# Fillers on TensorE moved from early pauses to later ones, written into the PSUM bank of the product that follows

## The chip, the cores and the metric

The kernel runs on one core of a Trainium2 chip. The metric is the device time of one execution in microseconds (us). Three timed runs of the kernel before gave 224.25, 225.02 and 223.09 us; their median is 224.25 us.

## The reference

Two blocks follow each other. The first is a linear attention with a sketched feature map, the second a phase mixer over tokens. Cut to what matters:

```python
# q, k, v: (4, 4, 1088, 32); S1, S2: (8, 32)
def phi(x):                       # 64 features of each row
    a = einsum('rd,bhsd->bhsr', S1, x); b = einsum('rd,bhsd->bhsr', S2, x)
    return einsum('bhsi,bhsj->bhsij', a, b).reshape(..., 64)
q_p, k_p = phi(q), phi(k)
kv  = einsum('bhsf,bhsd->bhfd', k_p, v);  z = k_p.sum(axis=2)
num = einsum('bhsf,bhfd->bhsd', q_p, kv); den = einsum('bhsf,bhf->bhs', q_p, z) + 1e-6
x = (num / den) heads put side by side    # (4, 1088, 128)

theta = x @ w_theta
zr, zi = x * cos(theta), x * sin(theta)
y = einsum('ts,bsd->btd', w_tok_r, zr) + einsum('ts,bsd->btd', w_tok_i, zi)
u = x + y
out = u + maximum(u @ w_ch, 0)            # (4, 1088, 128)
```

## The kernel before, in words

The kernel is written as a list of 1015 operations. Each has an engine (P for TensorE, V for VectorE, A for ScalarE, G for GpSimd, S for the queue of SyncE), the buffers that it writes and reads, and a function that issues its instructions. The order in which they are issued is written out by hand in `ORDER`, and the slot of every buffer in `PLACES`; nothing is planned at run time. Each engine works through its own operations in that order. An operation waits by semaphores for its operands and for the last reader of a slot that it takes over. PSUM has eight slots, `ps0` to `ps7`, each one bank of 512 float32 columns.

The work is staged by batch. Keys are transposed and turned into features (`kT`, `kf`), summed with the values (`kv`), and their Gram matrix (`sums`, `rest`) goes through a chain of small products (`chain`) that gives the scales for the exact slicing of the query side. `CHAINS` treats batch 0, batch 1, and batches 2 and 3 together. Queries are sliced (`q0`), multiplied (`levels`), divided by the denominator (`den`), brought to the output of the attention (`num`), and then the angles (`theta`) and the token mixing (`mix` for batches 0 and 1, `winograd` for 2 and 3) follow, then the last product and the stores (`out`). The token matrix arrives in 17 row blocks of float64 words, which ScalarE and VectorE turn into float32 (lines 555 to 561).

Fillers are matrix products on a tile of zeros, `idle`, whose result nobody reads. `spin` (line 349) issues one: bfloat16, 128 x 384, into the PSUM tile `nowhere` in slot `ps0`. Ten of them run at the start (line 353). `SPINS` names operations by their number and says how many fillers `issue` puts right ahead of each. One more filler is an operation of its own (line 1289): it waits for the key sums of batch 0, is the last that uses `nowhere`, and after it slot `ps0` goes to other tiles.

The operations that `SPINS` names in either version, all on TensorE:

| number | what it is | line of its instructions |
|---|---|---|
| 76 | transposes of the first key group, batch 0 | 694 |
| 89 | Gram matrix of the rounded keys, batch 0 | 637 (by 312) |
| 72 | key features, second group, batch 0 | 704 (by 312) |
| 303 | transposes of a query group, batch 0 | 918 |
| 111 | product with ones in the chain of batch 0 | 807 (by 312) |
| 172 | the product `second` in the chain of batch 1, into a tile `np` in `ps1` | 798 to 800 (by 312) |
| 174 | product with ones in the same chain, into a tile `pt` in `ps2` | 807 (by 312) |
| 1010 | last transpose of `finish_turned`, batch 2, into a tile `ut` in `ps5` | 1134 |

Line 312 is the helper `mm`, through which most products are issued. Around operation 172, TensorE's own order is: key features of batch 1 (141), then 172, transposes of the first query products of batch 0 (441, 439; line 1010), 174, key and value sums of batch 1 (144), the first numerators (443), further transposes and numerators, angles (459, 460) and, after 187, the levels of batch 1 (521). The operand of 172 is `tac`, which VectorE's operation 170 (line 788) and ScalarE's 171 (line 782) finish. At the end of the order stand 1006, 1010 and 1011 on TensorE, with copies on ScalarE (1007, 1012), the last additions on VectorE and the stores.

Of the kernel before, what the change touches and what calls it, by code (L numbers as in the profile page):

```python
# [9 lines left out]
F32 = mybir.dt.float32  # L10
# [11 lines left out]
P = 128  # L22
# [54 lines left out]
    "2 0 1 5 0 5 0 2 3 4 0 2 5 2 5 "  # L77
)
SPINS = (
    "76:2 89:4 72:2 303:1 111:2 "  # L80
)
WARM = 0
SPLIT = ()
# [35 lines left out]
class Layout:  # L119
# [5 lines left out]
    def buf(self, cls, shape, dt, name):  # L125
        b = Buf(cls, shape, dt, name)
        self.bufs.append(b)
        return b

    def op(self, eng, dur, fn, w=(), r=(), lk=0, fly=0.0, half=False, n=0):  # L130
        o = Op()
        o.n = n
        o.lk, o.fly, o.stage, o.half = lk, fly, self.stage, half
        o.i, o.eng, o.dur, o.fn = len(self.ops), eng, dur, fn
        pred = set()
        o.bufs = []

        def parts(x):
            return x if isinstance(x, tuple) else (x, None)

        def hits(table, b, key):
            t = table.get(b, {})
            return [v for k, v in t.items() if k is None or key is None or k == key]

        for x in r:
            b, key = parts(x)
            pred.update(hits(self.last_w, b, key))
            o.bufs.append(b)
        for x in w:
            b, key = parts(x)  # L150
            pred.update(hits(self.last_w, b, key))
            for s in hits(self.readers, b, key):
                pred.update(s)
            o.bufs.append(b)
        for x in r:
            b, key = parts(x)
            self.readers.setdefault(b, {}).setdefault(key, set()).add(o.i)
        for x in w:
            b, key = parts(x)
            if key is None:  # L160
                self.last_w[b] = {None: o.i}
                self.readers[b] = {}
            else:
                self.last_w.setdefault(b, {})[key] = o.i
                self.readers.setdefault(b, {})[key] = set()
        o.bufs = list(dict.fromkeys(o.bufs))
        for b in o.bufs:
            b.ops.append(o.i)
        pred.discard(o.i)
        o.pred = sorted(pred)  # L170
        self.ops.append(o)
        return o
# [10 lines left out]
    def issue(self, pools, fill):  # L183

        spins = dict(tuple(map(int, x.split(":"))) for x in SPINS.split())
        for o in self.order:
            for _ in range(spins.get(o.i, 0)):
                fill()
            for b in o.bufs:
                if b.ap is None:  # L190
                    b.ap = view(pools[b.cls](b.slot), b.shape, b.dt)
            o.fn()


WORD = {F32: 4, I32: 4, U32: 4, BF16: 2, F16: 2, I16: 2, I64: 8}
# [2 lines left out]
def view(raw, shape, dt):  # L198
    n = math.prod(shape)
    t = raw[:, : n * WORD[dt] // 4]  # L200
    if dt != F32:
        t = t.bitcast(dt)
    if len(shape) > 1:
        names = " ".join(f"a{i}" for i in range(len(shape)))
        t = t.rearrange(f"p ({names}) -> p {names}", **{f"a{i}": s for i, s in enumerate(shape)})
    return t
# [19 lines left out]
def kernel(  # L226
# [12 lines left out]
    B, _, NC, H, D = q.shape  # L239
# [13 lines left out]
    GW = GC * P  # L253
# [18 lines left out]
    def maker(c, width):  # L272
        pool = banks if c == "ps" else room
        return lambda i: pool.tile([P, width], F32, tag=f"{c}{i}", name=f"{c}{i}")

    pools = {c: maker(c, w) for c, (_, w) in classes.items()}
    L = Layout(classes)
    op, buf = L.op, L.buf
# [4 lines left out]
    V, A, G, T, SY = nc.vector, nc.scalar, nc.gpsimd, nc.tensor, nc.sync  # L283

    def fixed(shape, dt, name):
        b = Buf(None, shape, dt, name)
        n = math.prod(shape) * WORD[dt]
        b.ap = view(const.tile([P, (n + 3) // 4], F32, tag=name, name=name), shape, dt)
        return b
# [56 lines left out]
    idle = fixed((GW,), BF16, "idle")  # L346
    nowhere = buf("ps", (GW,), F32, "nowhere")

    def spin():
        T.matmul(nowhere(), idle()[:, 0:P], idle(), start=True, stop=True, skip_group_check=True)  # L350

    op("G", 0.3, lambda: G.memset(idle(), 0.0), [idle], [])
    op("P", 1.73, lambda: [spin() for _ in range(10)], [nowhere], [idle])
    op("V", 1.55, constants, [hm, bdm, halfpi, ups, steps, upv, ones], [])
    op("A", 0.72, lambda: A.activation(warm(), halfpi(), AF.Sin), [warm], [halfpi])
# [46 lines left out]
    def powers(mfn, m, n, name):  # L402
# [7 lines left out]
        def inv():  # L410
# [16 lines left out]
                                    op=ALU.max, apply_absolute_value=True), [m2], [(sp, 0)])  # L427
# [152 lines left out]
    kvb, kk, kg = {}, {}, {}  # L580
# [260 lines left out]
    def chain_out(bs):  # L841
        nu = nus[bs]
        at("kvb", bs[0])
        for n, b in enumerate(bs):
            mk = buf("sm", (H,), F32, "mk")
            ep[b] = (nu, n)
            op("V", 0.16, lambda n=n, mk=mk: tt(V, mk(), nu()[:, 0, n * H:(n + 1) * H], bde(), ALU.mult), [mk], [nu, bde])
            tr = buf("ps", (P,), F32, "kvtr")
            kt = kvb[b]
            bd = buf("sm", (H, D), F32, "kvbd")  # L850

            def twice(tr=tr, kt=kt):
                for n in range(2):
                    mm(tr()[n * R * R:(n + 1) * R * R], kt(), ident(), True, True)

            op("P", 0.31, twice, [tr], [kt, mk], half=True)
            vop(P, lambda bd=bd, tr=tr, mk=mk: tt(V, bd(), tr().rearrange("p (h d) -> p h d", h=H),
                                                  bc(mk(), 2, [P, H, D]), ALU.mult), [bd], [tr, mk])
            kvb[b] = bd
# [12 lines left out]
    def query_scale(b):  # L872
        at("qscale", b)
        x = ld["q", b]
        m = buf("sm", (3,), F32, "qm")
        n = NC * HD
        f = qx[b] = buf("big", (n,), F32, "qx")
        if QGRAM[b]:
            pq = buf("ps", (HW,), F32, "pq")
            dg = buf("sm", (HW,), F32, "qd")  # L880

            def gram():
                for c in range(NC):
                    y = x()[:, c].rearrange("p h d -> p (h d)")
                    for n in sides:
                        mm(pq()[n], y[:, n], y[:, n], c == 0, c == NC - 1)

            op("P", 1.05, gram, [pq], [x], half=True)
            op("V", 0.3, lambda: V.tensor_tensor_reduce(dg(), pq(), idh(), 1.0, 0.0, ALU.mult, ALU.add, m()[:, 0:1]),
               [dg, m], [pq, idh])  # L890
        else:
            op("A", act(n) + 0.1, lambda: A.activation(f(), x().rearrange("p c h d -> p (c h d)"), AF.Square,
                                                       accum_out=m()[:, 0:1]), [f, m], [x])
        t = buf("ps", (1,), F32, "qt")
        op("P", 0.25, lambda: mm(t(), ones(), m()[:, 0:1], True, True), [t], [m])
        s = qs[b] = fixed((2,), F32, f"qs{b}")

        def scale():
            a = m()[:, 1:2]
            ts(a, t(), QFIX, ALU.mult, TINY, ALU.max)  # L900
            ai = a.bitcast(I32)
            ts(ai, ai, 1, ALU.logical_shift_right, EXPO, ALU.bitwise_and)
            ts(ai, ai, EXPO, ALU.bitwise_xor)

        op("V", 0.53, scale, [m], [t])
        op("A", 0.2, lambda: A.mul(s()[:, 0:1], m()[:, 1:2], 2.0**-49), [(s, 0)], [m])
        small(lambda: ts(s()[:, 1:2], s()[:, 0:1], s()[:, 0:1], ALU.mult, ec()[:, 1:2], ALU.mult, eng=G), [(s, 1)],
              [(s, 0), (ec, 1)], dur=0.8)
# [372 lines left out]
    for bs in CHAINS:  # L1281
        for b in bs:
            kfeatures(b)
            key_sums(b)
            query_scale(b)
        chain(bs)
        chain_out(bs)
        if not bs[0]:
            op("P", 0.1, spin, [nowhere], [kvb[WARM]] if WARM < B else [idle])
    for b in range(B):  # L1290
        query_slices(b)
    for i in range(NK):
# [20 lines left out]
    with tc.manual_schedule():  # L1313
        L.issue(pools, spin)
# [43 lines left out]
```

## Time and profile before

| | before |
|---|---|
| timed runs, us | 224.25, 225.02, 223.09 (median 224.25) |
| profiled execution: time, us | 223.05 |
| profiled execution: span from first to last instruction, us | 221.3 |
| mean granted TensorE clock | 0.989 |
| TensorE busy, us | 212.6 (96%) |
| VectorE busy, us | 174.1 (79%) |
| ScalarE busy, us | 117.0 (53%) |
| fillers in the trace (line 350) | 22 |

The page calls TensorE's products PE and its weight loads PEld, VectorE DVE, ScalarE ACT, GpSimd POOL and SyncE SP. A line of a timeline gives the start, the duration, the engine, the line of the kernel, the operation, the tiles written and read, the shape, the number of instructions, and in brackets how long the engine had been idle before and who ended it. A tile that came from the class `big`, `g` or `sm` has that name. PEclk is the clock granted to TensorE, as a share of full speed. Products are pipelined, so a busy PE is not PE at its peak.

### The profile page before, as it was taken

Reading aid. Unit: us, or ns where it says so; the run is one execution under the profiler, and the core shown is the slowest. Engines: PE = TensorE matmul, PEld = TensorE weight load, DVE = VectorE, ACT = ScalarE, POOL = GpSimd, SP = SyncE. Lnnn points to the kernel's source line nnn. Section 1 sums busy time; section 2 is a strip of 40 time slices with the busy share of each in tenths; the row PEclk is TensorE's granted clock in tenths of the full one; section 3 lists DMA queues with packets and bytes.
Section 4 is the critical chain, followed back from the end, with each engine's and each line's share of the span. In section 5 each row is a group of like instructions: output and inputs, shape, how many; then the busy total and the mean of one; then the engine's idle time right before and its main releaser. Section 6 shows DMA issues by size and latency. Waiting matters only on the chain.

```text
span 221.3 us, 5085 instructions
## 1 busy us (share of the span) xinstructions
PE 212.6 (96%) x2047; PEld 160.2 (72%) x2047; DVE 174.1 (79%) x395; ACT 117.0 (53%) x228; POOL 22.2 (10%) x44
## 2 busy tenths in 40 slices
PE   7989997999998999999999999999999999999992
PEld 3777996776676676666668668767687888788882
DVE  4899999989989789879925955697379999893642
ACT  3998999889989944784415365604566000000000
POOL 2664000000033000001005030003000000000000
PEclk9999999699999999999999999999999999999998
DMA  5999579973577759659307234103200100022363
GB/s 178 416 417 413 185 292 422 428 306 110 184 273 190 193 198 351 256 201 300 116 0 121 89 76 90 18 1 59 39 0 0 30 3 0 0 36 41 65 97 76
DMA packets 23195, 34.68 MB, mean 157 GB/s; under 512 B 17028, under 2 KB 18308, under 8 KB 20996
## 3 DMA queue, kind: packets, MB, share of 16 engines
q1 hardware_dynamic: 17908, 29.28, 37.2%
q0 software_dynamic: 1728, 4.65, 9.7%
q10 hardware_dynamic: 3536, 0.43, 1.3%
q8 instruction: 16, 0.26, 0.5%
q14 instruction: 7, 0.06, 0.1%
HBM read 27.48 MB, written 2.23 MB: 134 GB/s over the span
## 4 chain that ended last, share of the span: by engine, by line
PE 79%; DMA 7%; DVE 7%; ACT 3%; issue 1%; SPq 1%; ACTq 0%
PE ps L312 71%; PE ps L1010 4%; DMA zs<-w_tok 3%; DMA big<-hf 3%; PE ps L918 2%; PE ps L1043 2%; DVE big L292 1%; ACT big L555 1%; ACT g L697 1%; DVE lv L292 1%; DMA out<-g 1%; DVE hf L296 1%; DVE sm L299 1%; DVE big L299 1%; DVE big L296 0%
## 5 line engine op out<-in xcount | busy, mean ns | idle before, releaser
L312 PE MATMUL ps<-big,zs 128*128 128x384 f32 (+4 forms) x398 | 110.8, 423 | 0.0
L312 PEld LDWEIGHTS ps<-big,zs 128*128 128x128 f32 x398 | 71.1, 190 | 27.8 <-issue 1.2
L1142 ACT COPY g<-ps 128x128 f32<-128x128 f32 (+1 forms) x3 | 0.9, 302 | 47.0 <-DMA out<-g 40.9
L312 PE MATMUL ps<-big,big 128*64 128x64 f32 (+2 forms) x208 | 21.7, 276 | 0.9 <-DMA big<-hf 0.8
L555 ACT ACTIVATE big<-zs 128x1088 f32<-128x1088 f32 x17 | 20.6, 1216 | 3.7 <-DVE big L292 3.6
L557 ACT ACTIVATE big<-zs 128x1088 int32<-128x1088 uint32 (+1 forms) x18 | 20.9, 1169 | 2.2 <-DVE big L292 2.2
L292 DVE CUSTOM_DVE_ANT_0 big<-big,big 128x2176 uint16<-128x2176 uint16 x17 | 21.8, 1285 | 0.4 <-ACT big L557 0.4
L312 PEld LDWEIGHTS ps<-big,big 128*64 128x64 f32 (+1 forms) x208 | 16.8, 154 | 4.3 <-issue 1.4
L292 DVE TENSOR_TENSOR big<-big,big 128x544 f32<-128x544 f32 x24 | 16.6, 715 | 0.7 <-PE ps L312 0.7
L292 DVE TENSOR_TENSOR zs<-ps,g 128x768 f32<-128x768 f32 (+2 forms) x20 | 12.3, 629 | 3.0 <-PE ps L1043 1.7
L306 POOL DMA_DIRECT2D big<-hf x6 | 5.4, 1000 | 86.5 <-DVE big L296 42.1
L296 DVE TENSOR_SCALAR big<-big 128x1088 int32<-128x1088 int32 x17 | 12.3, 724 | 1.5 <-ACT big L555 1.3
L292 DVE TENSOR_TENSOR g<-lv 128x768 f32<-128x768 f32 x12 | 11.2, 954 | 2.0 <-PE ps L312 1.7
L1014 ACT COPY g<-ps 128x384 f32<-128x384 f32 x24 | 10.2, 488 | 4.6 <-PE ps L1010 4.3
L312 PE MATMUL ps<-w,big 128*128 128x128 f32 x80 | 11.4, 279 | 0.0
L312 PEld LDWEIGHTS ps<-w,big 128*128 128x128 f32 x80 | 10.2, 192 | 1.1 <-issue 0.6
L299 DVE SCALAR_TENSOR_TENSOR g<-g,ps 128x384 f32<-128x384 f32 x12 | 6.4, 551 | 5.4 <-ACT g L1052 5.3
L1010 PEld LDWEIGHTS ps<-ident,g 128*128 128x128 f32 x72 | 8.9, 149 | 2.4 <-DVE sm L292 0.8
L1010 PE MATMUL ps<-ident,g 128*128 128x128 f32 x72 | 10.4, 287 | 0.1
L312 PE MATMUL ps<-g,sm 128*64 128x384 f32 x48 | 9.6, 516 | 0.0
L306 POOL DMA_DIRECT2D g<-big x6 | 5.7, 1008 | 35.2 <-ACT g L1120 35.2
L1055 ACT ACTIVATE g<-g 128x384 f32<-128x384 f32 x12 | 6.1, 520 | 5.4 <-DVE g L299 5.3
(185 smaller groups left out, 333.1 us busy)
## 6 DMA issues: line engine op xcount, KB each, us to landing
zs<-w_tok SPq DMA_DIRECT2D x17, 1088.0 KB, 5.1
big<-k_l SPq DMA_DIRECT2D x6, 576.0 KB, 4.8
big<-hf POOLq DMA_DIRECT2D x6, 576.0 KB, 5.0
big<-q_l SPq DMA_DIRECT2D x4, 576.0 KB, 8.6
big<-v_l SPq DMA_DIRECT2D x4, 576.0 KB, 13.6
g<-big POOLq DMA_DIRECT2D x4, 192.0 KB, 3.0
out<-g SPq DMA_DIRECT2D x16, 48.0 KB, 1.9
g<-big POOLq DMA_DIRECT2D x2, 160.0 KB, 3.4
```

Of the source, the lines that this page charges most:

```text
L292: eng.tensor_tensor(out=o, in0=a, in1=b, op=f)
L296: (eng or V).tensor_scalar(out=o, in0=a, scalar1=s1, scalar2=s2, op0=op0, **kw)
L299: (eng or V).scalar_tensor_tensor(out=o, in0=a, scalar=s, in1=b, op0=op0, op1=op1)
L306: op("G", 0.9, lambda: G.dma_start(dst(), src(), accum_op=ALU.add), w, r, fly=fly)
L312: T.matmul(o, lhs, rhs, start=start, stop=stop, skip_group_check=True)
L555: op("A", 0.22 + n * 0.0009, lambda: A.activation(dfn(), words_of(raw(), n)[1].bitcast(F32), AF.Prelu, scale=2.0**-112, alpha=-(2.0**32)), ...
L557: op("A", 0.22 + n * 0.0009, lambda: A.activation(stp(), words_of(raw(), n)[0].bitcast(U32), AF.Copy, scale=2.0**-29), [stp], [raw])
L918: T.transpose(tr()[:, i * P:(i + 1) * P], x()[:, g * GC + i].rearrange("p h d -> p (h d)"), ident())
L1010: T.transpose(tr()[:, i * P:(i + 1) * P], qp()[:, i * H + 2 * n:i * H + 2 * n + 2].rearrange("p h i j -> p (h i j)"), ident())
L1014: op("A", act(GW), lambda n=n, tr=tr, qT=qT: A.copy(qT()[:, n], tr()), [(qT, n)], [tr])
L1043: T.transpose(x()[:, i], xs()[:, off + i * P:off + (i + 1) * P], ident())
L1055: op("A", act(GW), lambda cs=cs: A.activation(cs()[:, 0], cs()[:, 1], AF.Abs), [(cs, 0)], [(cs, 1)])
```

## The change

Two early fillers go (one of four before operation 89, one of two before 72), and ten come: eight before 172, one before 174 and one before 1010. Since slot `ps0` belongs to other tiles by then, a filler issued after the operation of line 1289 writes into the PSUM tile that the operation behind it takes over and overwrites. To that end `issue` takes the tile first and issues the fillers after it. The order of the operations and the slots stay the same.

```diff
 SPINS = (
-    "76:2 89:4 72:2 303:1 111:2 "
+    "76:2 89:3 72:1 303:1 111:2 172:8 174:1 1010:1 "
 )
...
         spins = dict(tuple(map(int, x.split(":"))) for x in SPINS.split())
+        shared = True
         for o in self.order:
-            for _ in range(spins.get(o.i, 0)):
-                fill()
+            n, home = spins.get(o.i, 0), None
+            if shared:
+                for _ in range(n):
+                    fill()
             for b in o.bufs:
                 if b.ap is None:
-                    b.ap = view(pools[b.cls](b.slot), b.shape, b.dt)
+                    raw = pools[b.cls](b.slot)
+                    home = raw if b.cls == "ps" else home
+                    b.ap = view(raw, b.shape, b.dt)
+            if not shared:
+                for _ in range(n):
+                    fill(home)
             o.fn()
+            shared = shared and o is not self.parted
...
-    def spin():
-        T.matmul(nowhere(), idle()[:, 0:P], idle(), start=True, stop=True, skip_group_check=True)
+    def spin(home=None):
+        T.matmul(nowhere() if home is None else view(home, (GW,), F32), idle()[:, 0:P], idle(), start=True, stop=True, skip_group_check=True)
...
         if not bs[0]:
-            op("P", 0.1, spin, [nowhere], [kvb[WARM]] if WARM < B else [idle])
+            L.parted = op("P", 0.1, spin, [nowhere], [kvb[WARM]] if WARM < B else [idle])
```

## The prediction

> **What bounds the kernel now.** I read the page first (shares, slices, chain), then busy time and granted clock in stretches of 3.41 us, then the timelines of PE and DVE around the edits.
>
> ```profile
> PE 212.6 (96%) x2047; PEld 160.2 (72%) x2047; DVE 174.1 (79%) x395; ACT 117.0 (53%) x228; POOL 22.2 (10%) x44
> ...
> PE   7989997999998999999999999999999999999992
> ...
> PEclk9999999699999999999999999999999999999998
> ...
> PE 79%; DMA 7%; DVE 7%; ACT 3%; issue 1%; SPq 1%; ACTq 0%
> ```
>
> PE bounds: 96% busy, 79% of the chain that ended last. One slice has a low clock, the eighth (38.7 to 44.3 us). The stretches place it:
>
> ```profile
> 31.92:35.33 3.41, 3.34 (x71) 2.88 (x74) 3.41 (x8) 3.00 (x9) 0.00 (x0) 1.00 1.04 439
> 35.33:38.74 3.41, 1.83 (x54) 1.63 (x42) 3.34 (x12) 3.29 (x8) 0.00 (x0) 1.00 0.98 407
> 38.74:42.16 3.42, 3.37 (x38) 2.64 (x37) 3.30 (x10) 2.58 (x4) 0.00 (x0) 0.50 1.04 436
> ...
> 69.46:72.88 3.42, 2.63 (x77) 2.34 (x76) 3.39 (x6) 3.39 (x8) 1.74 (x2) 1.00 0.63 154
> ```
>
> After the clock, the columns are PE, PEld, DVE, ACT, POOL, granted clock. A stretch with PE busy 1.83 of 3.41 is followed by one at half clock; one with 2.63 keeps 1.00. The pause and the slow work, on PE:
>
> ```profile
> 35.56 0.92 PE L312 MATMUL ps<-sbk,g 128*64 128x64 f32 x24
> 38.06 0.84 PE L312 MATMUL ps<-sm,pbd 128*128 128x64 f32 x6 [1.58 <-ACT big L710]
> 38.95 1.51 PE L1010 MATMUL ps<-ident,g 128*128 128x128 f32 x6
> ...
> 42.56 1.53 PE L1010 MATMUL ps<-ident,g 128*128 128x128 f32 x12
> ```
>
> The product at 38.06 is operation 172, before which eight fillers now go. Six transposes at half clock take what twelve take at full clock. The releaser named is not the true one: the product's last operand is DVE's instruction of 37.73 that ends at 37.91, below.
>
> **The change, part by part.** *Eight fillers before 172.* Four earlier fillers show the price:
>
> ```profile
> 7.29 0.81 PE L350 MATMUL ps<-idle 128*128 128x384 bf16 x4
> 8.04 0.47 PE L312 MATMUL ps<-hf 128*64 128x64 bf16 x18
> 8.44 0.50 PE L350 MATMUL ps<-idle 128*128 128x384 bf16 x2
> ...
> 9.94 0.28 PE L312 MATMUL ps<-big,big 128*64 128x64 f32 x2 [0.16 <-DVE big L292]
> ```
>
> One lasts 0.326 us and the next begins 0.163 later: (0.81 - 0.326) / 3 = 0.16. Eight are 8 x 0.163 = 1.30, with the last one's tail 1.47. Their bank's former content, a transposed key block, was read by ACT by 35.15, so they start when PE is free, at 36.48 at the latest, and are through by 37.95. The product's operand arrives at 37.91 and its weights begin loading at 38.03: added delay 0, at most 0.1. The wait that now ends on the fillers has only the same product behind it.
>
> What they bring: the stretch to 38.74 holds 1.83 + 1.30 = 3.13 of 3.41, more than the 2.63 that kept the clock, so I take it that the clock stays at 1.00 to 42.16. Half clock for 3.41 us costs PE at most 1.71 us. How much comes through is counted step by step. The six transposes still begin at 38.95 and are spaced 0.109 instead of 0.213; their last starts at 39.50, not 40.05. ACT's two copies of them, which now wait until 40.50, start near 39.81, so the four products behind them start at 40.72, not 41.42; they then take 0.70 instead of 1.14, and the twelve transposes of 42.56 start at 41.50. PE is 1.06 ahead. But DVE must follow:
>
> ```profile
> 37.73 0.18 DVE L292 TENSOR_TENSOR sm<-sm,sm 128x32 f32<-128x32 f32 x1
> ...
> 40.73 0.16 DVE L296 TENSOR_SCALAR sm<-ps 128x4 f32<-128x4 f32 x1
> ...
> 44.43 0.17 DVE L296 TENSOR_SCALAR mv<-sm 128x32 f16<-128x32 f32 x1
> 45.32 0.56 DVE L299 SCALAR_TENSOR_TENSOR g<-g,ps 128x384 f32<-128x384 f32 x1 [0.72 <-ACT g L1052]
> ...
> 46.45 0.19 DVE L292 TENSOR_TENSOR mv<-sm,mv 128x32 f16<-128x32 f32 x1
> ```
>
> From 37.85 to 46.64 DVE stands idle only for 0.09 before 40.73, 0.13 before 42.48 and 0.72 before 45.32: 0.94 in all, and it can be no earlier than that. The 0.72 waits for ACT, which waits for PE's products of 43.93; these move up by 1.0, so the instruction of 45.32 starts near 44.42. The level products of 46.62 need the slice that DVE ends at 46.64 and move up by **0.9**.
>
> Does 0.9 reach the end? DVE has no gap from 45.32 to 65.14 and PE none from 38.95 to 70.10, so both carry it. At 70.89 PE waits 0.79 for a transfer that POOL issues behind DVE's rounding of 62.07; that moves along. Afterwards PE waits for nothing until 216.78. The thinnest cover is the product at 95.96, whose weights DVE ends at 95.56: 0.40. DVE sat waiting for PE just before these, at 94.13, so they move too; if they did not, 0.4 would be left. Bounds: 0.4 and 1.71; I take 0.9, where the counted rows lead.
>
> [...]
>
> *One filler before 174* (line 807). Its bank was last read by DVE's instruction of 38.72, over at 39.67, and the product's operand, the reduction of 39.59, is over at 39.77. The filler runs about 39.75 to 39.91 in a pause that the faster transposes open (39.61 to 39.9). If the clock dropped after all, there is no pause and it costs 0.16 to 0.33. DVE, which reads the result, is busy until 40.64 either way. I take 0.
>
> *One filler before 1010*, the next to last transpose group. PE is free at 216.62 and the transpose waits for DVE until 216.78; a filler of 0.163 fits in the 0.21 before 216.83. If it comes late it costs up to 0.1 straight on the final chain. I take 0.
>
> *One filler fewer before 89 and 72.* Each operation may start 0.16 earlier (the first waits for DVE until 7.77, fillers hold it to 8.03). Behind them PE waits at 9.94 for DVE, so the 0.33 becomes idle time there: 0. ACT's copy of the result sits behind its own work until 9.72, so at most 0.1 comes through. Cover gone, the price is a clock drop (a rival below).
>
> **Sum.** The profiled execution has span 221.3 and time 223.05; with -0.9 they become 220.4 and 222.15. That execution is faster than all three timed runs (223.09, 224.25, 225.02). Since I can't see what the slower ones lose, I carry the difference to the median: 224.25 - 0.9 = **223.3 us**.
>
> **Rivals.** *The drop is not there to be cured, or not cured.* If the clock is judged in fixed stretches, a pause of 1.58 cut by their border leaves 0.79 in each, as much as the stretch with 2.63 busy that kept its clock; such runs have no drop before and gain nothing. The same time follows if fillers count too little as work. For it: the three runs differ by 1.9 us. Against it: the ten fillers at the start lie 0.32 apart and the next ones 0.16, so a stretch of fillers alone raised the clock. Time: 224.25.
>
> *More comes through.* If ACT and DVE follow closer than counted, or the slower runs lose more to the same pause, all of 1.71 returns: 222.5. Against it: DVE's 0.94 of idle time.
>
> *A new drop early: slower.* Two fillers fewer leave up to 0.49 idle before 9.94, and 12.59 to 13.09 is idle already. A stretch of 3.41 can hold 0.77 of both, while 0.79 kept the clock and 1.58 lost it. If the limit lies at 0.77, PE runs at half clock for 3.41 us from about 13: it loses 1.71, less the idle 0.25 between 16.3 and 19.6 that hides a part, 1.45, and PE is on the chain from 16.43. With the later gain kept: 224.25 - 0.9 + 1.45 = 224.8; without it 225.7. This decides only if the limit is just below what the trace has seen held.
>
> **Chances.** Forecast 0.55, nothing gained 0.22, more comes through 0.11, early drop 0.12. A measurement of this kernel tells about 1% (2.2 us) from no change, and every case's center lies within that. Runs scatter by 1 us around the median: the third case passes 222.0 in half its outcomes and the forecast in a tenth, together 0.11; the early drop passes 226.5 in a third, with a little from scatter 0.06; the rest, 0.83, is within 1%. The range runs from all the loss returned with some scatter, 222.1, to the early drop's middle, 225.0.
>
> **What would show it.** Right: fillers of line 350 number 30, not 22; eight in a row from about 36.4; the clock row without the 6; six transposes from 38.95 in 0.82; the level products near 45.7; the wait of 0.79 for the transfer still there; PE's order otherwise as before. Wrong: a half-clock stretch at another place (above all between 11 and 20 us), the product of 38.06 starting later, DVE's gap of 0.72 still open, or an end that has not moved though the clock held.

## The result and the profile after

The changed kernel takes **222.37 us** in the median of 13 runs (221.82 to 223.15), the kernel before 223.82 beside it (13 runs, 222.98 to 225.48). The ratio is 0.9935, interval 0.9909 to 0.9962: a gain of 0.65%, real, and less than the 1% that the chances were stated by. The profiled execution of the changed kernel, 223.15 us with a span of 221.4, is the longest of its 13 and must not be set beside the 221.3 of before without looking at what it lost. The page, shares and slices as before:

```profile
PE 212.4 (96%) x2055; PEld 159.8 (72%) x2055; DVE 173.9 (79%) x395; ACT 116.6 (53%) x228; POOL 22.8 (10%) x44
...
PE   7999997899998999999999999999999999999993
...
PEclk9999999999999999999999999999999999999998
...
PE 79%; DVE 8%; ACT 6%; DMA 4%; issue 1%; POOL 0%; POOLq 0%
```

The digit 6 is gone from the clock row, and the eight products more (2055, not 2047) are the fillers: 30, not 22. The same stretches as shown of before (columns: length, busy PE, PEld, DVE, ACT, POOL, granted clock, DMA share, GB/s):

```profile
35.33:38.74 3.41, 2.33 (x39) 1.48 (x32) 3.17 (x10) 2.13 (x2) 0.00 (x0) 1.00 0.99 411
38.74:42.16 3.42, 2.70 (x43) 2.26 (x43) 2.67 (x6) 3.42 (x10) 0.00 (x0) 1.00 1.05 440
69.46:72.88 3.42, 2.45 (x76) 2.27 (x75) 3.39 (x6) 3.39 (x8) 1.74 (x2) 1.00 0.64 153
```

The second row has clock 1.00 where it had 0.50. But the first holds 2.33 of work, not the 3.13 that the prediction put there. PE's and ScalarE's timelines say why (all lines of the source are nine higher than before: L350 is now L359, L312 L321, L1010 L1019):

```profile
36.18 1.47 PE L359 MATMUL ps<-idle 128*128 128x384 bf16 x8
39.14 0.85 PE L321 MATMUL ps<-sm,pbd 128*128 128x64 f32 x6 [1.49 <-ACT sm L791]
39.83 0.85 PE L1019 MATMUL ps<-ident,g 128*128 128x128 f32 x6
40.52 0.33 PE L359 MATMUL ps<-idle 128*128 128x384 bf16 x1
...
46.62 0.57 PE L321 MATMUL ps<-mv,hf 128*64 128x96 f16 x18
```

```profile
36.61 1.20 ACT L564 ACTIVATE big<-zs 128x1088 f32<-128x1088 f32 x1 [1.69 <-DMA zs<-w_tok]
37.72 1.16 ACT L566 ACTIVATE big<-zs 128x1088 int32<-128x1088 uint32 x1
38.78 0.30 ACT L791 ACTIVATE sm<-sm,kg 128x32 f32<-128x32 f32 x1
```

The eight fillers take the predicted 1.47 and end at 37.65. The product behind them starts at 39.14, 1.08 later than before, and not because of them: it is idle for 1.49 more. ScalarE, which makes an operand of it, stood 1.69 us for a row block of the weights. The last sixteenth of that block landed at 36.58 (34.23 before), while the fifteenth was there by 34.05. So one late part of a transfer took in this execution what the held clock gave, about 1.06, and the level products start at 46.62 in both kernels. An execution without the late part follows below.

**What the mean clock says of every run.** Each run lists its mean granted clock. A stretch of 3.41 us at half clock lowers the mean over 221 us by 0.5 x 3.41 / 221 = 0.0077, so the mean counts the lowered stretches. The time before the clock's first rise does not enter the mean: in before it first rose at 4.61, and the mean of 0.989 is 1 - 0.5 x (3.41 + 1.61) / 221.3. The 1.61 us stand behind the last product, where the clock is down once more, in before from 219.65 to the end of the span, in the changed kernel's profile from 219.86 (1.50 us); that takes 0.0036 and 0.0034. What it takes differs with the rise (in the profiles without a lowered stretch, a rise at 4.3 to 4.8 us leaves 0.996 to 0.999, one at 5.0 to 7.2 leaves 0.999 to 1.000). Of 108 runs of before (those beside the experiments and the first experiment):

| mean clock | lowered stretches | runs of before | median us |
|---|---|---|---|
| 0.984 to 0.985 | two | 23 | 225.06 |
| 0.988 to 0.992 | one | 82 | 223.75 |
| 0.997 to 0.998 | none | 3 | 222.21 |

The changed kernel in 25 runs (13, and 12 in an experiment): 0.995 to 1.000 in all of them, median 222.46. So none of them lost the stretch.

### The profile page after: what moved, and what is told of

It reads as the page before. It is cut to its first block, busy times and chain, and to the rows that moved or that the text cites. A ratio compares the mean times of both kernels' runs of the same rounds, so it can differ in the third digit from the quotient of the medians.

```text
span 221.4 us, 5101 instructions
## 1 busy us (share of the span) xinstructions
PE 212.4 (96%) x2055; PEld 159.8 (72%) x2055; DVE 173.9 (79%) x395; ACT 116.6 (53%) x228; POOL 22.8 (10%) x44
## 4 chain that ended last, share of the span: by engine, by line
PE 79%; DVE 8%; ACT 6%; DMA 4%; issue 1%; POOL 0%; POOLq 0%
PE ps L321 70%; PE ps L1019 3%; DMA big<-hf 3%; PE ps L359 2%; PE ps L1052 2%; ACT g L706 1%; PE ps L927 1%; DVE g L301 1%; ACT big L566 1%; DVE big L301 1%; DVE lv L301 1%; PE ps L703 1%; DMA out<-g 1%; DVE hf L305 1%; DVE sm L308 1%
## 5 line engine op out<-in xcount | busy, mean ns | idle before, releaser
L321 PE MATMUL ps<-big,zs 128*128 128x384 f32 (+4 forms) x398 | 110.8, 423 | 0.0
L321 PEld LDWEIGHTS ps<-big,zs 128*128 128x128 f32 x398 | 71.1, 190 | 27.8 <-issue 1.2
L321 PE MATMUL ps<-big,big 128*64 128x64 f32 (+2 forms) x208 | 21.7, 276 | 1.5 <-DMA big<-hf 1.0
L321 PEld LDWEIGHTS ps<-big,big 128*64 128x64 f32 (+1 forms) x208 | 16.8, 154 | 4.8 <-issue 1.6
L321 PE MATMUL ps<-w,big 128*128 128x128 f32 x80 | 11.4, 279 | 0.0
L321 PEld LDWEIGHTS ps<-w,big 128*128 128x128 f32 x80 | 10.2, 192 | 1.1 <-issue 0.6
L1019 PEld LDWEIGHTS ps<-ident,g 128*128 128x128 f32 x72 | 8.4, 143 | 2.0 <-DVE g L301 0.8
L1019 PE MATMUL ps<-ident,g 128*128 128x128 f32 x72 | 9.8, 274 | 0.0
L321 PE MATMUL ps<-g,sm 128*64 128x384 f32 x48 | 9.3, 501 | 0.3 <-ACT g L1023 0.3
L359 PE MATMUL ps<-idle 128*128 128x384 bf16 x30 | 8.1, 393 | 1.3 <-POOL idle L361 1.3
```

Source lines behind the costliest of these rows:

```text
L321: T.matmul(o, lhs, rhs, start=start, stop=stop, skip_group_check=True)
L359: T.matmul(nowhere() if home is None else view(home, (GW,), F32), idle()[:, 0:P], idle(), start=True, stop=True, skip_group_check=True)
L1019: T.transpose(tr()[:, i * P:(i + 1) * P], qp()[:, i * H + 2 * n:i * H + 2 * n + 2].rearrange("p h i j -> p (h i j)"), ident())
```

## The experiments

All are timed against before in five rounds, and differ from the kernels shown in the string `SPINS` alone. The ratios stand as recorded; they are not always those of the two medians. The theory: the pause ahead of operation 172 costs the clock of the next stretch, and eight fillers save it. The rivals: the cut of early fillers, or the fillers ahead of 174 and 1010, do the work; or the clock has nothing to do with it.

**1. The kernel before, against itself.** No edit.

> The kernel before itself, unchanged, to see clock and span of each of its runs. My theory (the pause ahead of operation 172 costs a half-clock stretch, and one late row of the token matrix costs another 0.9 us in some runs) expects a ratio of 1.000 and granted clocks near 0.985 to 0.99 in nearly every run, with times in steps: near 223.1 where the row is in time, 224.0 and above where it is late. The rival, that the pause is mostly cut by the border of a stretch and so seldom costs anything, expects clocks of 0.995 and above in a good part of the runs, and those among the fastest, near 222.2.

Measured: 223.62 (222.90 to 224.27), ratio 0.997 (0.9944 to 0.9996). Two sets of the same kernel on one chip differ by 0.3%, so differences of 0.3 to 0.6 us below are at the edge of what can be told.

**2. Eight fillers before 172, nothing else.**

```diff
-    "76:2 89:4 72:2 303:1 111:2 "
+    "76:2 89:4 72:2 303:1 111:2 172:8 "
```

> Only the eight fillers ahead of operation 172; the early fillers as before, none ahead of 174 and 1010. My theory, that these eight are the whole gain, expects 0.9935 (222.4 us), clock 0.995 or above in all runs, product of 172 not delayed by them. The rival, that cutting two early fillers brings the gain, expects 1.000.

Measured: 223.29 (222.71 to 225.43), ratio 0.998 (0.9947 to 1.0013): not the 0.9935 that the theory expected, and not 0.995 or above in all runs. Nine of 12 runs have no lowered stretch (222.71 to 224.16), three have one (0.989 to 0.990) and take 225.3. So the fillers before 172 do most of what holds the clock, but the time hardly followed. In the profiled execution (clock 1.00 throughout) the level products start at 45.93, 0.7 before the 46.62 of before, though the clock rose later (6.33, not 4.61), and POOL issues the two transfers of the join (the product at 70.89 in before waits for them) 0.7 earlier too, at 62.94; yet the last of their parts lands at 71.00, against 70.76 before:

```profile
71.14 1.27 PE L321 MATMUL ps<-big,big 128*64 128x64 f32 x36 [1.73 <-DMA big<-hf]
```

The wait that was 0.79 is now 1.73: in this execution the gain was given back there. The other eleven runs have no profile.

This wait is also a test of what lowers the clock. In steps of 3.413 us, the length of the lowered stretch of before, counted from the clock's rise, it lies whole within one stretch, a longer pause than the 1.58 of before, and the stretch behind it keeps clock 1.00:

```profile
67.77:71.18 3.41, 1.68 (x42) 1.02 (x41) 3.36 (x7) 3.38 (x8) 1.74 (x2) 1.00 0.61 145
71.18:74.59 3.41, 3.41 (x45) 2.62 (x46) 2.24 (x3) 2.95 (x5) 0.00 (x0) 1.00 1.05 261
```

With PE busy 1.68 of 3.41 the clock was kept, where 1.83 lost it ahead of operation 172. So PE's busy share, as the profile has it, does not decide by itself.

**3. The cut of the early fillers alone.**

```diff
-    "76:2 89:4 72:2 303:1 111:2 "
+    "76:2 89:3 72:1 303:1 111:2 "
```

> Only the two early fillers fewer; no later fillers. My theory expects 1.000 within 0.3%: the 0.33 us turn into idle time ahead of the product that waits for VectorE near 10 us. The rival that the cut brings the gain expects 0.9935. The rival of a new half-clock stretch early expects 1.003 or more and a clock row below 9 between 11 and 20 us.

Measured: 224.28 (222.13 to 224.62), ratio 0.999 (0.9961 to 1.0019): nothing that can be told from no change, as the sum had it. One run has no lowered stretch, nine have one, two have two. The profiled one is of the last kind:

```profile
34.86:38.27 3.41, 1.83 (x61) 1.56 (x55) 3.34 (x11) 3.29 (x8) 0.00 (x0) 1.00 1.00 413
38.27:41.68 3.41, 3.41 (x40) 3.22 (x40) 3.14 (x7) 2.43 (x6) 0.00 (x0) 0.50 1.03 428
41.68:45.10 3.42, 3.42 (x14) 2.24 (x15) 2.88 (x9) 2.40 (x5) 0.00 (x0) 0.50 1.02 414
```

The pause leaves 1.83 of work, as before, and here the clock is half for two stretches, though PE is busy all through the first of them. No half clock stands between 11 and 20 us, where the prediction's third rival feared it.

**4. The two single fillers, before 174 and 1010, alone.**

```diff
-    "76:2 89:4 72:2 303:1 111:2 "
+    "76:2 89:4 72:2 303:1 111:2 174:1 1010:1 "
```

> Only the single fillers ahead of 174 and 1010; the early fillers as before, none ahead of 172. My theory expects 1.000 to 1.002: the one ahead of 174 costs 0.16 to 0.33 us of TensorE time at half clock, partly hidden, the one ahead of 1010 fits in its pause. If the last filler sits on the final chain, up to 0.1 us more.

Measured: 223.60 (222.01 to 224.76), ratio 0.9973 (0.9942 to 1.0003), below the 1.000 to 1.002 expected but no more than before differs from itself. Three of 12 runs have no lowered stretch, eight one, one two. The profiled one is of the first kind, with the whole pause of 1.58 still open (37.23 to 38.81). Its stretches:

```profile
34.46:37.87 3.41, 2.71 (x82) 2.23 (x80) 3.34 (x10) 3.00 (x6) 0.00 (x0) 1.00 0.98 395
37.87:41.28 3.41, 2.41 (x39) 2.13 (x39) 3.41 (x8) 3.12 (x9) 0.00 (x0) 1.00 1.00 413
```

The clock rose to 1.00 at 7.15 in this execution and at 4.61 in that of before. Counted on in steps of 3.413 us, a border falls at 37.87, inside the pause, and each side keeps 2.4 or more of work. In before the borders are 35.33 and 38.74, and the pause lies whole between them. So the same pause does not always lower the clock: cut by a border it did not, and the grid stood elsewhere in each profile (the clock rose at 4.14 to 7.16). That is the prediction's first rival, seen at work in this one profile, though the second stretch holds the filler before 174 too. Whether it is also what spared the three of 108 runs of before is not shown: their mean clock, 0.997 to 0.998, points to an early rise, and this execution's is 1.000.

**5. Early cut and eight fillers before 172; none before 174 and 1010.**

```diff
-    "76:2 89:4 72:2 303:1 111:2 "
+    "76:2 89:3 72:1 303:1 111:2 172:8 "
```

> Early fillers cut as in the change (89:3 72:1) and eight fillers ahead of 172; none ahead of 174 and 1010. Theory A (the clock is judged in stretches of 3.413 us on a grid that every execution starts elsewhere, and the one filler ahead of 174 is needed where a border of that grid falls between 38 and 41 us): most runs without a lowered stretch at 222.2 to 223.2, about a quarter with one (mean granted clock near 0.99) at 224.4 to 225.4, as in the run with eight ahead of 172 alone. Rival B (what that run lacked against the change was the early cut): all runs without a lowered stretch, median 222.4, ratio to before 0.993 to 0.994.

Measured: 222.59 (221.99 to 223.53, 9 runs), ratio 0.9934 (0.9908 to 0.996), all nine at 0.995 or more. The whole gain is there without the fillers before 174 and 1010, as rival B had it; theory A's quarter of lowered runs did not show. The profiled execution, 223.05, has the same late weights as the changed kernel's (the row block landed at 36.48, the product started at 39.03).

**6. Early fillers as before, the new ones all there.**

```diff
-    "76:2 89:3 72:1 303:1 111:2 172:8 174:1 1010:1 "
+    "76:2 89:4 72:2 303:1 111:2 172:8 174:1 1010:1 "
```

> Early fillers as before (89:4 72:2), and eight ahead of 172, one ahead of 174, one ahead of 1010. Theory A: no run has a lowered stretch, since the filler ahead of 174 is there; median 222.4 to 222.9, ratio 0.993 to 0.996, and what is left to the change's 222.4 is the price of the two early fillers where the clock is released late. Rival B: the early fillers matter: median 223.3, a quarter of the runs with a lowered stretch at about 225.3, ratio 0.998.

Measured: 222.89 (222.53 to 223.51), ratio 0.996 (0.9938 to 0.9983), none of 12 with a lowered stretch. It is 0.3 above experiment 5 on the same chip, which has the cut but not the two single fillers. Theory A's range holds; rival B's quarter of lowered runs did not show. The profiled execution loses as experiment 2 did: the level products start at 46.29 here and at 46.33 in experiment 11, whose clock rose at nearly the same time (7.14 here, 7.04 there), and POOL issues the join at 63.29 and 63.33; but the join's last part lands at 71.32 and 70.69. PE's wait, first here, then in experiment 11:

```profile
71.46 1.23 PE L321 MATMUL ps<-big,big 128*64 128x64 f32 x35 [1.69 <-DMA big<-hf]
```

```profile
70.82 1.27 PE L321 MATMUL ps<-big,big 128*64 128x64 f32 x36 [1.02 <-DMA big<-hf]
```

The spans are 221.7 and 221.1: the whole difference. Both profiles with uncut early fillers and eight before 172 show this late last part, but so does that of experiment 8, where they are cut. Whether the cut matters to a transfer 60 us later is not settled.

**7. Four fillers before 172 in place of eight.**

```diff
-    "76:2 89:3 72:1 303:1 111:2 172:8 174:1 1010:1 "
+    "76:2 89:3 72:1 303:1 111:2 172:4 174:1 1010:1 "
```

> The change with four fillers ahead of 172 in place of eight. The stretch that was half idle would hold 1.83 + 4 x 0.18 = 2.6 us of work of 3.41, where one with 2.63 kept the clock before. Theory A (the share of busy time in the stretch decides): the clock holds in nearly all runs, median 222.4 to 222.7, ratio 0.993 to 0.995. Rival B (a pause has to be filled whole, or the one left, 0.85 us, is enough for a drop in some phases): a third or more of the runs with a lowered stretch at 223.1 to 224.2, median about 223.2, ratio 0.997.

Measured: 222.07 (221.83 to 222.90, 6 runs), ratio 0.9928 (0.99 to 0.9957), no lowered stretch: rival B is out. The pause need not be filled whole.

**8. Sixteen fillers.** The same edit with `172:16`.

> The change with sixteen fillers ahead of 172. Sixteen at 0.184 us, the mean of the eight in the changed kernel's profile, take 2.9 us from 36.2 and end at 39.1, where the product could start at 38.06 if the last row block of the weights is on time: 1.05 us later. Theory A (what is late at 172 comes out at the end, by about 0.9): no lowered stretch, median 222.4 + 0.9 less what late weights hide in some runs, 222.9 to 223.3, ratio 0.996 to 0.998. Rival B (the delay ends in the wait for the join's transfer, which hides it): as the change, 222.4, ratio 0.9935.

Measured: 223.67 (223.19 to 225.31), ratio 0.9996 (0.9972 to 1.002); 11 of 12 runs without a lowered stretch. The clock is held in those, and the gain is gone; the loss is a little more than theory A's 222.9 to 223.3. PE in the profiled execution:

```profile
37.04 2.77 PE L359 MATMUL ps<-idle 128*128 128x384 bf16 x16
39.65 0.75 PE L321 MATMUL ps<-sm,pbd 128*128 128x64 f32 x6
```

In experiment 6, whose clock rose within 0.15 us of this one's (7.14 and 6.99), the product starts at 38.75. It is 0.90 late here, the level products 0.61 (46.90), the join's last part 0.78 (72.10), the span 0.79, the median 0.78 (1.08 above experiment 5, which has the cut as this one has). The join's wait did not hide it (1.85 here, 1.69 there): rival B is out, and most of what is late at 172 reaches the end. The late weight block in the profile of the changed kernel made the same product late by 1.08; no run tests a late block by itself.

**9. Two fillers.** The same edit with `172:2`.

> The change with two fillers ahead of 172. The stretch that was half idle would hold 1.83 + 2 x 0.2 = 2.2 us of work of 3.41, 0.65: between 1.83, which lost the clock, and about 2.6, which kept it. Theory A (share of the stretch decides, limit somewhere between 0.54 and 0.75): either nearly all runs hold the clock and the median is that of four fillers, 222.1 to 222.4, or most have one lowered stretch and it is 223.1 to 223.8; the mean granted clock of the runs tells which. Rival B (any pause left of over a microsecond loses the clock): one lowered stretch in nearly all runs, 223.6.

Measured: 222.00 (221.83 to 224.13), ratio 0.9957 (0.9927 to 0.9986). Nine of 12 runs have no lowered stretch (221.83 to 222.83), three have one (0.990 to 0.991; 223.52 to 224.13). In the profiled execution, of the nine, a pause of 1.14 is left, whole within one stretch:

```profile
35.25:38.66 3.41, 2.27 (x48) 1.68 (x36) 3.34 (x12) 3.30 (x8) 0.00 (x0) 1.00 1.01 421
38.66:42.07 3.41, 3.28 (x45) 2.30 (x45) 3.38 (x11) 3.24 (x7) 0.00 (x0) 1.00 1.01 421
```

Its grid lies within 0.1 us of that of before. Here a stretch with 2.27 of work kept the clock where 1.83 lost it, so rival B is out; but with three of 12 runs lowered, two fillers are not safe. The changed kernel's own profiled execution has a smaller one: cut at its grid (the clock rose at 4.82), the stretch 35.54 to 38.96 holds 2.12, and kept it.

**10. No fillers before 76, 89 and 72.**

```diff
-    "76:2 89:3 72:1 303:1 111:2 172:8 174:1 1010:1 "
+    "303:1 111:2 172:8 174:1 1010:1 "
```

> The change with no fillers at all ahead of 76, 89 and 72, where it has six left (2, 3 and 1). Theory A (the early fillers cost only where the clock is released late, where each takes 0.4 in place of 0.16): lowest run as the change's, 221.8 to 222.0, upper runs some 0.3 lower, median 222.0 to 222.3, no lowered stretch. Rival B (they hold up the release or the clock in their own stretch, 4 to 11 us): lowered or late stretches at the start, median 223 to 225.

Measured: 222.58 (221.89 to 223.48), ratio 0.9955 (0.993 to 0.998), no lowered stretch. Beside experiment 11 on the same chip (222.59) the remaining six early fillers neither cost nor save anything that can be told. The 0.3 of theory A did not show, and rival B is out.

**11. The change itself**, beside 9, 10 and 12.

> The change itself, beside the others of this chip: no lowered stretch, median 222.2 to 222.7, ratio to before 0.992 to 0.996.

Measured: 222.59 (222.05 to 223.00), ratio 0.9961 (0.9939 to 0.9983), no lowered stretch.

**12. Four fillers again**, beside the change.

> Four fillers ahead of 172 once more, beside the change on one chip. Theory A (eight fillers cost nothing that four do not, since the product waits for ScalarE's copies in both): the same as the change within 0.3 us. Rival B (eight fillers end within 0.2 us of the product's start and push it where its inputs are early): 0.2 to 0.5 us below the change.

Measured: 222.19 (221.92 to 222.85), ratio 0.9947 (0.9922 to 0.9972), no lowered stretch: 0.4 below the change, outside theory A's 0.3 and within rival B's range, but no more than before against itself. Rival B's push is in no profile: in experiments 2, 6, 10 and 11, with eight fillers and the weights in time, PE stands idle for another 0.17 to 0.18 between the fillers and the product (in experiment 11 from 38.61 to 38.78). A part of the 0.4 is where the clock rose: ten of the 12 runs of experiment 11 have a mean clock of 1.000, six of these 12, and in both the runs at 1.000 are the slower ones (medians 222.68 against 222.20 there, 222.52 against 221.98 here). The profiles agree: with the weights in time and the clock held, the level products start at 45.28 to 45.58 where it rose at 4.4 to 5.0 (experiments 7, 9, 12) and at 46.25 to 46.35 where it rose at 7.0 to 7.2 (experiments 4, 6, 10, 11). The profiled execution of experiment 12 (221.93) is the like of before's that the changed kernel's was not: PE reaches the pause at the same time and the weights land in time.

```profile
36.49 0.82 PE L359 MATMUL ps<-idle 128*128 128x384 bf16 x4
38.03 0.83 PE L321 MATMUL ps<-sm,pbd 128*128 128x64 f32 x6 [0.72 <-ACT big L719]
38.92 0.84 PE L1019 MATMUL ps<-ident,g 128*128 128x128 f32 x6
...
41.52 1.53 PE L1019 MATMUL ps<-ident,g 128*128 128x128 f32 x12
...
69.83 1.27 PE L321 MATMUL ps<-big,big 128*64 128x64 f32 x36 [0.78 <-DMA big<-hf]
```

```profile
40.52 0.15 DVE L305 TENSOR_SCALAR sm<-ps 128x4 f32<-128x4 f32 x1
...
43.99 0.18 DVE L305 TENSOR_SCALAR mv<-sm 128x32 f16<-128x32 f32 x1
44.27 0.55 DVE L308 SCALAR_TENSOR_TENSOR g<-g,ps 128x384 f32<-128x384 f32 x1
```

Against before: the product at 38.03 (38.06), the six transposes 0.84 long (1.51), the twelve 1.04 earlier, VectorE's product 1.05 earlier with its gap of 0.72 closed but for 0.10, the level products at 45.58 (46.62), the join's product 1.06 earlier behind the same wait (0.78, was 0.79), the last transpose at 215.76 (216.83), the span 1.1 shorter (220.15, was 221.26). Of all this, 0.03 is there already at the product behind the fillers.

## Why the prediction was right, and where its sizes were off

*The eight fillers fit and delay nothing.* Right: 1.47 with the tail, as counted, and over before the product's inputs are there, in every profile with eight. The product's later start in the changed kernel's profile, which the text had put down as a sign of error, came from ScalarE's late weights. In the four profiles with eight fillers and the weights in time 0.17 to 0.18 was left; sixteen fillers show what a real push costs.

*The clock holds.* Right, in all 25 runs, but the reason given is not enough. The text took the 2.63 of the stretch at the join as work that keeps the clock; at the same place 1.68 kept it in experiment 2 and 1.72 in experiment 6 (68.58 to 71.99), and near the end 1.83 did in experiment 10 (215.37 to 218.78), while 1.83 ahead of 172 lost it. So the row set no limit for the stretch of operation 172. That filling this pause saves the clock is shown by the runs; what the clock weighs besides PE's busy time is open. The stretch that lost it is made up of products of 64 columns, the one that kept it at 1.68 of the end of six products of 384 columns and 36 of bfloat16; no run separates these. A pause of 1.58 was enough to lose the clock in before and experiment 3, and the same length kept it in experiment 4. That the clock changes in fixed stretches, which the prediction's first rival only supposed, fits the trace of before: it rose at 4.609 and fell at 38.742, ten steps of 3.413 later, and stayed low for 3.413.

*PE 1.06 ahead, VectorE's cap 0.94, 0.9 to the end.* The mechanism was right and the term too small: 1.05 at VectorE's product, 1.06 at the join, 1.07 at the last transpose. The term that was mis-sized is the cap. It added up idle time from the end of one VectorE record to the start of the next, but back-to-back records overlap by 0.09 (in experiment 12 one starts at 37.82 and takes 0.96, to 38.78, and the next starts at 38.69). So each of the three gaps was worth 0.09 more, 1.2 in all. The first two gave it (0.18 and 0.22 in experiment 12); at the third VectorE still waits 0.10, so PE's 1.06 was the bound.

*0.9 through to the end, the wait for the join moving along.* Right in experiment 12, in both halves. Not always: in experiments 2 and 6 the join's last part lands late and keeps 0.7 to 0.9 of the gain.

*The median.* 223.3 was forecast, 222.37 measured; 0.93 apart. Some 0.4 is the base: 224.25 was the median of three runs, one of which, 225.02, has a time of the group with two lowered stretches; 108 runs give 223.9. Some 0.15 is the cap. The rest is what the longer runs lose, which the text said it could not see: over all runs the group with one lowered stretch lies 223.75 - 222.46 = 1.3 above the changed kernel, and about a fifth of before's executions lose two. So the time came out near the low end of the range, and the part of it that is the base is chance. Within those that lose one, 28 runs at 0.988 to 0.989 have a median of 223.1 and 38 at 0.991 to 0.992 one of 224.1; the profiled executions of before (0.989, the clock risen at 4.61) and of experiment 1 (0.988) are of the first kind, and what the drop costs in the second was in no profile. The second kind has the means of a later rise, and a rise at 7 in place of 4.4 to 5.0 puts the level products 0.7 to 1.1 later without any drop (experiment 12), so it need not lose more to the drop itself.

*The filler before 174, the one before 1010, the early cut: 0.* The last stands at 216.79 in the changed kernel's profile, between products, and experiment 5 has the full gain without both. In experiment 4 three of 12 runs escape the drop, three of 108 without them: the filler before 174 may help in some positions of the grid, which the text did not see and no profile settles. The cut is 0 alone, and PE's idle time before the products of 9.94 grows from 0.16 to 0.48 as counted; in company it may be worth 0.3, but experiments 5 and 6 differ in the two single fillers too, and that stays open.

*The rivals.* A drop moved to the start occurred in no profile. "More comes through" is nearest to the result in its time, 222.5, but not in its reason: in the like executions (before, experiment 12) 1.06 and not 1.71 came back of one stretch, and some executions of before lost a second.

Three things stay open: what the clock weighs besides PE's busy time; the three runs of experiment 2, and one of experiment 8, at 225.3 with one lowered stretch, whose place no profile caught; and why the clock stays half for a second stretch in some executions though the first is busy throughout.

## What to carry to other kernels

Where a tensor clock drops, cut the trace at the moments at which the clock changed and look at whole stretches, not at the length of pauses alone. Then test a few counts of fillers: four did here what eight did, two did not always, and sixteen pushed the work behind them. A busy share that kept the clock in one place of this kernel (1.68 of 3.41 at the join) was no limit for another (1.83 lost it ahead of 172). Take the mean clock of every timed run before believing one profile, since it tells how often the event happens, and compare executions whose clock rose at the same time. When reading how much slack a follower engine has, measure its gaps against how its records overlap when it is busy (0.09 us on VectorE here).

## What the runs showed of the hardware

- The clock changed on a grid of 3.413 us that began elsewhere in each profile: it rose at 4.14 to 7.16 us, and fell a whole number of steps later (10 and, at the end, 63 in before; 63, at the end, in the changed kernel).
- Ahead of operation 172 a stretch with PE busy 1.83 of 3.41 lost the clock of the next one (before, experiment 3); 2.12, 2.27 and 2.41 kept it (the changed kernel, experiments 9 and 4). At the join 1.68, with a pause of 1.73 in one piece, kept it too (experiment 2). Neither the pause nor the busy share in the profile decided alone.
- After a fall the clock stayed half for one stretch (3.41 us in before) or for two (6.83 us in experiment 3). The mean clock of 23 of 108 runs of before is that of two lowered stretches.
- Where the clock rose later, the work far behind it was later: the level products started at 45.28 to 45.58 with a rise at 4.4 to 5.0 (experiments 7, 9, 12) and at 46.25 to 46.35 with one at 7.0 to 7.2 (experiments 4, 6, 10, 11).
- One sixteenth of a transfer landed well after the others: at 36.58 against 34.05 for the fifteenth of the weights in the changed kernel, where ScalarE stood 1.69 us for it. Of the join's transfer the last part landed 0.56 after the twelfth in before and 0.68 in the changed kernel; its product started 7.2 to 7.5 us after POOL's issue in before, the changed kernel and experiments 7, 10, 11 and 12, and 8.2 to 8.3 after it in experiments 2, 6 and 8.
